# Token sums of a gated layer made in place, from the tile that the multiplication filled

## The chip, the cores and the metric

The kernel runs on one core of one Trainium2 chip. The metric is the time of one execution in microseconds (us); lower is better. Three runs of the kernel before gave 828.37, 828.44 and 830.95 us, median 828.44.

## The reference, cut to what matters

An attention over 32 memory slots for 4 batches of 576 tokens is followed by two feed-forward layers. All is float32.

```
x = attn_out as [2304 tokens, 512]
a = x @ w_a ; b = x @ w_b          # 512 -> 1536
x = (a * b) @ w_out                # 1536 -> 512   "the projection"
h = x @ w_in                       # 512 -> 2048
g = h * sigmoid(1.702 * h)
out = g @ w_out2                   # 2048 -> 512
```

The change is in what happens to `a * b` between its multiplication and the projection.

## The kernel before

**Engines and order.** TensorE (PE) does all products, each float32 operand split into a high and a low part and multiplied in three passes. ScalarE (ACT) and VectorE (DVE) empty the PSUM banks and decode weights (which come as raw 64-bit words); GpSimd (POOL) does elementwise sums beside DVE; SyncE (SP) issues nearly all DMAs. A planner (`Order`) runs while the program is built: it keeps a clock for each engine and for the DMA, starts from durations in `Lengths`, and writes each engine's instructions in the order in which its plan has them. Each engine, SP too, then works its list strictly in that order: an instruction that waits holds up all behind it.

**The gated layer** (`fold`, `gated`, `gated_out`). The 1536 columns are 6 groups `g` of 256, two blocks `j` of 128 each. For each group and batch, `fold` (L771) makes the effective weights; `gated` (L819) multiplies each half `u` (288 tokens) of the batch; ACT copies `a` from PSUM into a tile `gr` (L838), DVE multiplies `b` into it (L841), and SP stores the tile, 128 x 2 x 288, to a DRAM tensor `g1d` (L846). There are 24 pairs of group and batch and so 48 such stores. `gr` has four tiles of half a batch each.

**The token sums** (`sum_kept`, `sum_tokens`). The projection is one level of Strassen's scheme: 7 products in place of 8, over 2 x 2 blocks; one direction of the blocks is `j`, the other is a split of the tokens. The blocks of the token side are b11, b12, b21, b22; the products use b11, b21, b22 as they are, and four sums T1 to T4 of them. Before, the token split is between two stretches of 384 tokens within 768 (three such periods `p`). From the mark `close` on (the end of attention, near 142 us) `sum_kept` loads 2 x 768 tokens of a group from `g1d` into one of two tiles in `acc` (L924), POOL makes the four sums in place (L936), and SP stores them to `g1t` (L937). There are 18 such rounds. A load waits until its tile is free, that is until the store of the round two before it has landed.

**The projection** (`load_kept`, `split_kept`, `project`). For each period and product SP loads the block from `g1d` or `g1t` (L963), ACT and DVE or POOL split it into high and low parts, and PE multiplies (L1002). The weights for it come from `w_out`, of which 12 pieces are loaded into raw tiles (L360), decoded by ACT (L426) and DVE (L428, L430, L434), and combined (`combine_out`). Two raw tiles, `raw_74` and `raw_75` in the program, serve all weights after the end of attention.

**After it**: `w_in` (L1279), the gate, `w_out2` (L1480 and L1511).

Of the kernel before, what the change touches and what calls it, by code (L numbers as in the profile page):

```python
# [34 lines left out]
PS1 = 14.8  # L35
PT1 = 15
PB1 = 4
PI = 9
# [41 lines left out]
def pool(n):  # L80
    return 150 + 2.1 * n
# [18 lines left out]
class Order:  # L100
# [9 lines left out]
    def __init__(self):  # L110
        self.clock = {PE: 0.0, ACT: 0.0, DVE: 0.0, POOL: 0.0}
        self.dma, self.marks, self.streams, self.count = 2000.0, {}, [], 0

        self.handicap = {DVE: W0}

    def mark(self, t, *key):
        self.marks[key] = t

    def load(self, t, size, *key):

        self.dma = max(self.dma, t) + size / 385.0
        self.mark(self.dma + 2000.0, *key)

# [61 lines left out]
def tile_mem_attention_moe_moe2(  # L185
# [58 lines left out]

    g1d = dram.tile([F1, NT], F32, name="g1d")
    g1t = dram.tile([4 * F1 // 2, NT // 2], F32, name="g1t")
    g2d = dram.tile([F2, NT], F32, name="g2d")
# [5 lines left out]
    raw_s = slots(wp, 2, [P, 512, 2], "raw", U32)  # L253
    raw_t = list(raw_s.free)
    raw_x = slots(pa, 1, [P, 512, 2], "raw_x", U32)
# [7 lines left out]
    def y_of(p):  # L263
# [15 lines left out]
    ]  # L279
    gr_s = Slots([  # L280
        p2_m[:, o:o + G1 * U].rearrange("p (j t) -> p j t", j=G1)
        for o in range(B * HG * M, B * HG * M + 4 * G1 * U, G1 * U)
    ])
    rg_s, ring_s, sums_s, hc_s = Slots(), Slots(), Slots(), Slots()
    o1_s = {c: Slots() for c in range(F1 // P)}
# [59 lines left out]

    def raw_of(i):
        return raw_x if i == 2 * NHG - 1 else raw_s

# [358 lines left out]
    def close_attention():  # L707

        for n in range(NU):
            for e in range(2):  # L710
                yield "mark", "attn", n, e
        yield "mark", "raw_p"
        for i in range(4):
# [8 lines left out]
        four[0], four[1], four[2] = *views(spare, 4 * DM, 2), acc[:, 10 * DM:14 * DM]  # L722
        spare = views(spare, DM, NA * G1 + 2 * NHG)
        for c in range(NA * G1):
            give(o1_s[c], spare[c:c + 1])
        for r in range(2 * NHG):
            give(home[4, r], spare[NA * G1 + r:NA * G1 + r + 1])
        od.mark(now(), "close")

    py, pw, big = None, None, {}  # L730

    def room_late():

        for i in range(NA // 2):
            yield "mark", "w1", i
        yield "mark", "fold", 4, B - 1
        nonlocal pw
# [59 lines left out]
    def gated(g, b, u):  # L797
# [4 lines left out]
        e = eff_t[g, b][0]  # L802
        gr = yield "slot", gr_s
        left, pt, wide = [], [], have("close")
# [28 lines left out]
    def gated_out(g, b, u, j, pt, gr, left):  # L833
        (ta, pa_), (tb, pb) = pt
        n = j.stop - j.start
        xa, xb = (x[0][:, :, :U] if n > 1 else x[0][:, :U].rearrange("p (i t) -> p i t", i=1) for x in (pa_, pb))
        t, _ = yield ACT, max(ta, gr[1]), act(n * U, True)
        nc.scalar.activation(out=gr[0][:, j], in_=xa, func=AF.Copy)  # L838
        (pair_s if n > 1 else bank_m).release(pa_, t)
        t, _ = yield DVE, max(t, tb), dve(n * U)  # L840
        nc.vector.tensor_tensor(out=gr[0][:, j], in0=xb, in1=gr[0][:, j], op=ALU.mult)  # L841
# [68 lines left out]

    def kept(g, o, n):
        t = 0.0
        for i in range(o // U, (o + n - 1) // U + 1):
            t = max(t, (yield "mark", "g1", g, i // 2, i % 2))
        return t

    def sum_kept():

        yield "mark", "close"
        last = [(4, 0), (4, 1), (5, 0), (4, 2), (5, 1), (5, 2)]  # L920
        for g, p in [(g, p) for g in range(NG1 - 2) for p in range(NP)] + last:
                s = yield "slot", sums_s
                t = max(s[1], (yield from kept(g, 2 * p * N2, 2 * N2)))
# [4 lines left out]
                od.load(t, CW * 2 * N2 * 4, "kept", p, g)  # L928
                od.spawn(PT1 + 8 * p, sum_tokens(p, g, s))

    def sum_tokens(p, g, s):
        t = yield "mark", "kept", p, g
        b11, b12, b21, b22 = (s[0][:, i] for i in range(4))
        for dst, in0, in1 in ((b11, b12, b11), (b12, b22, b12), (b22, b22, b11), (b21, b21, b22)):
            t, _ = yield POOL, t, Lengths.pool * pool(N2)
            nc.gpsimd.tensor_tensor(out=dst, in0=in0, in1=in1, op=ALU.subtract)  # L936
        nc.sync.dma_start(  # L937
            out=g1t.rearrange("(x g p) t -> g p x t", g=NG1, p=P)[g][:, :, p * N2:(p + 1) * N2], in_=s[0]
        )
        sums_s.release(s, t + 2500.0)  # L940
        od.mark(t + 2500.0, "sums", p, g)

    def load_kept():

        for p in range(NP):
            for name in STEPS:
                b = PRODUCTS[name][1]
                for q in range(NG1 // 2):
                    s = yield "slot", rg_s
                    t = s[1]  # L950
                    for g in (2 * q, 2 * q + 1):
                        if b in PLAIN:
                            j, u = PLAIN[b]
                            o = (2 * p + u) * N2
                            t = max(t, (yield from kept(g, o, N2)))
                        else:
                            t = max(t, (yield "mark", "sums", p, g))
                    if b in PLAIN:
                        src = g1d.rearrange("(g j p) t -> j p g t", j=G1, p=P)[j]
                    else:  # L960
                        o = p * N2
                        src = g1t.rearrange("(x g p) t -> x p g t", g=NG1, p=P)[TSUM[b]]
                    nc.sync.dma_start(out=s[0], in_=src[:, 2 * q:2 * q + 2, o:o + N2])  # L963
                    od.load(t, CW * N2 * 4, "rg", p, name, q)
                    loaded["rg", p, name, q] = s
# [54 lines left out]
    def product_out(t, p, r, name, ps):  # L1020
# [13 lines left out]
        if p == 1:  # L1034
            for g in range(NG1):
                t = max(t, (yield "mark", "sums", NP - 1, g))
        mb = 2 * half + r
# [28 lines left out]
    WK, WB = NA * 2 * NB, 7 * (NG1 - NA) * 2 * NB + 128  # L1066
    PLAIN = {B11: (0, 0), B21: (1, 0), B22: (1, 1)}
    TSUM = {T1: 0, T3: 1, T4: 2, T2: 3}
    yc, win, wo2 = {}, {}, []
# [3 lines left out]
    def views(m, n, count, o=0):  # L1073
        return [m[:, o + i * n:o + (i + 1) * n] for i in range(count)]
# [18 lines left out]
    def room_weights():  # L1093

        yield "mark", "first"
        tiles = [x.rearrange("p (i t) -> p i t", i=4) for x in views(acc, 4 * N2, 2)]
        give(sums_s, tiles)
        yield "mark", "fold", 2, B - 1
# [20 lines left out]
    def room_buffers():  # L1119

        for b in range(B):
            for g in range(NG1):
                for u in range(2):
                    yield "mark", "g1", g, b, u
        give(hc_s, views(p2_m, N2, 7))
# [430 lines left out]
    def store(i, src, queues=(nc.sync,)):  # L1556

        for n, t in enumerate(range(i * P, (i + 1) * P, QP)):
            b, r = divmod(t, S)
            e, c = divmod(r // QP, QC // 2)  # L1560
# [17 lines left out]
    def main():  # L1578
# [4 lines left out]
        for p in range(NP):  # L1583
            yield from project(p)
        yield from quad(*order[0])
        room_projected()
        od.spawn(6, load_gated())
# [17 lines left out]
    with tc.manual_schedule():  # L1605
# [18 lines left out]
        od.spawn(9, room_weights())  # L1624
        od.spawn(3, sum_kept())
        od.spawn(3, load_kept())
# [39 lines left out]
```

## Time and profile before

| | |
|---|---|
| median of three runs | 828.44 us |
| the profiled execution | 830.54 us, of which the span of the profile is 828.7 us |
| PE busy | 763.5 us, 92% of the span |
| DVE, ACT, POOL busy | 609.5, 394.3, 378.5 us |
| moved by DMA | 171.23 MB, mean 207 GB/s |
| granted TensorE clock, mean | 0.965 |

Busy shares are averages over stages with different limits, so they say little alone. The stages are: attention with the first gated work (to 104 us), gated work with nothing in its way (104 to 142), gated work with the token sums and the weights of the projection (142 to 307), the start of the projection (307 to 344.4), and the rest.

### The profile page before, as it was taken

How to read it: one execution, taken by the hardware profiler on the slowest of the kernel's cores; microseconds unless marked ns; L12 is line 12 of the kernel's file. 1: busy time of each engine (PE TensorE's matmuls, PEld its weight loads, DVE VectorE, ACT ScalarE, POOL GpSimd, SP SyncE). 2: the span in 40 equal slices, each digit the busy share in tenths (PEclk: the TensorE clock that was granted, in tenths of full speed). 3: DMA queues.
4: the chain of work that ended last, by engine and by line, in shares of the span. 5: the costliest groups of instructions: out<-in, count | busy, mean ns of one | idle time of the engine just before them, and what ended most of it. 6: DMA issues, size and time to landing. Idle time of an engine off the chain costs nothing.

```text
span 828.7 us, 14577 instructions
## 1 busy us (share of the span) xinstructions
PE 763.5 (92%) x5360; PEld 701.3 (85%) x5360; DVE 609.5 (74%) x920; ACT 394.3 (48%) x781; POOL 378.5 (46%) x326
## 2 busy tenths in 40 slices
PE   8899999977876875799999999999999999999997
PEld 7667788766655775799999999999999888899997
DVE  4888987554765565359659897776778779999884
ACT  3565654322443242356466556555455446544441
POOL 0211100534656285539348977322214009887661
PEclk9999999988988987999999999999999999999999
DMA  8987735778766688975666255644457995754411
GB/s 255 314 273 237 247 122 162 257 260 264 261 207 207 205 311 273 319 245 167 199 187 185 62 172 207 195 166 161 155 194 263 298 316 186 231 168 131 130 33 40
DMA packets 115160, 171.23 MB, mean 207 GB/s; under 512 B 8592, under 2 KB 89232, under 8 KB 115088
## 3 DMA queue, kind: packets, MB, share of 16 engines
q1 hardware_dynamic: 109632, 160.89, 60.4%
q10 hardware_dynamic: 5456, 9.41, 3.3%
q8 instruction: 42, 0.69, 0.3%
q14 instruction: 30, 0.25, 0.1%
HBM read 114.16 MB, written 56.10 MB: 205 GB/s over the span
## 4 chain that ended last, share of the span: by engine, by line
PE 59%; DMA 16%; DVE 8%; POOL 8%; issue 4%; ACT 3%; SPq 2%; ACTq 0%; DVEq 0%; POOLq 0%
PE bank L1279 17%; PE bank L1511 12%; PE bank L1480 11%; PE bank L1002 10%; PE bank L819 5%; DMA g1t<-acc 4%; DMA raw<-in_moe_w_out_dram 4%; DMA raw<-in_moe_w_b_dram 3%; POOL acc L328 2%; POOL w L328 2%; DMA acc<-g1d 1%; POOL acc L936 1%; POOL w1b L328 1%; DMA phi<-in_phi_dram 1%; POOL attn L328 1%
## 5 line engine op out<-in xcount | busy, mean ns | idle before, releaser
L819 PEld LDWEIGHTS bank<-attn,eff 128*128 128x128 f32 x1152 | 166.2, 201 | 55.1 <-ACT gr L838 21.1
L819 PE MATMUL bank<-attn,eff 128*128 128x288 f32 x1152 | 179.3, 313 | 32.0 <-ACT gr L838 18.3
L936 POOL TENSOR_TENSOR acc<-acc 128x384 f32<-128x384 f32 x72 | 80.4, 1132 | 111.7 <-DMA acc<-g1d 109.8
L328 POOL TENSOR_TENSOR acc<-acc 128x512 f32<-128x512 f32 (+2 forms) x64 | 94.7, 1502 | 44.4 <-DVE w L328 25.6
L328 DVE TENSOR_TENSOR w<-acc,w 128x512 fp32r<-128x512 f32 (+2 forms) x101 | 103.8, 1055 | 11.1 <-ACT w L334 11.1
L1321 DVE TENSOR_TENSOR acc<-bank,acc 128x384 f32<-128x384 f32 x168 | 88.4, 550 | 31.6 <-PE bank L1279 19.8
L1002 PE MATMUL bank<-attn,w 128*128 128x384 f32 x504 | 97.1, 346 | 13.5 <-ACT attn L334 10.1
L1002 PEld LDWEIGHTS bank<-attn,w 128*128 128x128 f32 x504 | 90.8, 195 | 16.8 <-ACT attn L334 10.7
L334 ACT ACTIVATE w<-acc 128x512 fp32r<-128x512 f32 (+2 forms) x129 | 74.8, 590 | 56.1 <-PE bank L1511 37.1
L328 DVE TENSOR_TENSOR attn<-acc,attn 128x768 fp32r<-128x768 f32 (+3 forms) x59 | 72.8, 1248 | 35.1 <-ACT attn L334 34.6
L334 ACT ACTIVATE attn<-acc 128x768 fp32r<-128x768 f32 (+2 forms) x80 | 61.1, 768 | 54.9 <-PE bank L1002 27.0
L1331 ACT ACTIVATE acc<-acc 128x384 f32<-128x384 f32 x96 | 48.3, 521 | 47.6 <-DVE acc L1321 47.1
L328 POOL TENSOR_TENSOR attn<-acc,attn 128x768 fp32r<-128x768 f32 (+2 forms) x21 | 35.9, 1720 | 46.2 <-ACT attn L334 46.2
L1279 PE MATMUL bank<-attn,w 128*128 128x384 f32 x288 | 55.3, 334 | 0.7 <-POOL attn L328 0.7
L1279 PEld LDWEIGHTS bank<-attn,w 128*128 128x128 f32 x288 | 50.3, 188 | 1.1 <-POOL attn L328 1.1
L841 DVE TENSOR_TENSOR gr<-bank,gr 128x288 f32<-128x288 f32 (+1 forms) x64 | 38.4, 599 | 15.4 <-PE bank L819 12.8
L1002 PE MATMUL bank<-attn,w1b 128*128 128x384 f32 x252 | 47.9, 336 | 1.2 <-ACT attn L334 0.6
L426 ACT ACTIVATE acc<-raw 128x512 f32<-128x512 f32 x27 | 18.3, 678 | 61.3 <-DMA raw<-in_moe_w_b_dram 34.8
L838 ACT ACTIVATE gr<-bank 128x288 f32<-128x288 f32 (+1 forms) x64 | 33.6, 526 | 27.2 <-PE bank L819 26.8
L1279 PE MATMUL bank<-w1b,w 128*128 128x384 f32 x224 | 46.2, 334 | 0.0
L1002 PEld LDWEIGHTS bank<-attn,w1b 128*128 128x128 f32 x252 | 43.8, 188 | 2.3 <-DVE attn L328 1.4
L328 POOL TENSOR_TENSOR w<-acc,w 128x256 fp32r<-128x256 f32 (+2 forms) x26 | 28.4, 1102 | 36.0 <-ACT w L334 36.0
(177 smaller groups left out, 1456.5 us busy)
## 6 DMA issues: line engine op xcount, KB each, us to landing
g2d<-acc SPq DMA_DIRECT2D x96, 192.0 KB, 2.3
raw<-in_moe_w_out_dram SPq DMA_DIRECT2D x28, 512.0 KB, 5.3
g1d<-gr SPq DMA_DIRECT2D x48, 288.0 KB, 5.4
acc<-g1d SPq DMA_DIRECT2D x18, 768.0 KB, 4.8
g1t<-acc SPq DMA_DIRECT2D x18, 768.0 KB, 6.7
acc<-g1t SPq DMA_DIRECT2D x36, 384.0 KB, 3.7
acc<-g1d SPq DMA_DIRECT2D x27, 384.0 KB, 4.0
acc<-g2d SPq DMA_DIRECT2D x10, 1024.0 KB, 6.4
```

The lines of the kernel that those rows point to most:

```text
L328: (nc.gpsimd if e == POOL else nc.vector).tensor_tensor(out=dst, in0=in0, in1=in1, op=op)
L334: nc.scalar.activation(out=hi, in_=src, func=AF.Copy)
L819: nc.tensor.matmul(dst[:, :U], e[:, c, sw, i * CW + j * P:i * CW + (j + 1) * P], attn(b, mv, c, u * U, U), start=(n == 0), stop=(n == 3 * ...
L838: nc.scalar.activation(out=gr[0][:, j], in_=xa, func=AF.Copy)
L841: nc.vector.tensor_tensor(out=gr[0][:, j], in0=xb, in1=gr[0][:, j], op=ALU.mult)
L936: nc.gpsimd.tensor_tensor(out=dst, in0=in0, in1=in1, op=ALU.subtract)
L1002: nc.tensor.matmul(ps[0][:, :N2], w1_of(a, g, sw)[:, r * P:(r + 1) * P], b[0][:, mv, i], start=(first and q == n == 0), stop=(q == NG1 // ...
L1279: nc.tensor.matmul(ps[0][:, :N2], w[:, sw, r, :], y[mv][r], start=(n == 0), stop=(n == 5))
L1321: nc.vector.tensor_tensor(out=s[0], in0=ps[0][:, :N2], in1=x[0], op=ALU.add)
L1331: nc.scalar.activation(out=c[0], in_=c[0], func=AF.Gelu_apprx_sigmoid)
L1480: nc.tensor.matmul(ps[i, s][0], b[0][:, sw, c - o, :], wo2[c][:, mv], start=(c == n == 0), stop=(c == 4 * K4 - 1 and n == 2),)
L1511: nc.tensor.matmul(ps[name][0][:, :NB], x[0][:, sw, c, :], moving(b, h // 2 + c, mv), start=(h == c == n == 0), stop=(h > 0 and c == K4 - ...
```

## The change

The token blocks are now the two halves `u` of each batch: b11 and b12 are the two halves of block `j` = 0, b21 and b22 those of block `j` = 1. A tile `gr` holds both halves of a batch, 128 x 4 x 288, so that all four blocks of a group and batch stand side by side in it. After each half SP stores what the products use as it is: both blocks of the first half, and only b22 of the second (L869 of the changed kernel). Then POOL makes the four sums in that same tile (L884), and SP stores them (L885). `sum_kept` with its loads, and `g1t`, are gone; all seven blocks lie in `g1d`, 1152 tokens wide, and periods are stretches of 384 of those.

There are four tiles of a whole batch: two in the old place and two in the attention's pool, which are given up at its end (`gr_x`); two more come in `acc` when the first group is folded. Every third piece of `w_out` gets a third raw tile in `spare` (`raw_z`). The planner counts stores on its DMA clock too, and from `close` to the end of the projection it uses 330 bytes per ns and 3000 ns to landing (`RATE`) in place of 385 and 2000. The rows of the final stores follow the new token order.

```diff
+    gr_m = [p2_m[:, o:o + 4 * U] for o in range(B * HG * M, B * HG * M + 4 * G1 * U, 4 * U)]
+    gr_p = [pa.tile([P, 4 * U], F32, name=f"grp{i}") for i in range(2)]
+    gr_s = Slots([x.rearrange("p (i t) -> p i t", i=4) for x in gr_m + gr_p])
+    gr_x = list(gr_s.free[2:])
...
     def raw_of(i):
+        if pieces[i][0][0] == "o1" and i % 3 == 0:
+            return raw_z
...
-            o = b * S + u * U
+            lo, n = ((0, G1), (3, 1))[u]
             nc.sync.dma_start(
-                out=g1d[g * CW:(g + 1) * CW, o:o + U].rearrange("(j p) t -> p j t", p=P), in_=gr[0]
+                out=g1v[2 * u:2 * u + n, :, g, b * U:(b + 1) * U].rearrange("x p t -> p x t"),
+                in_=gr[0][:, lo:lo + n],
             )
-            gr_s.release(gr, t + 2500.0)
-            od.mark(t + 2500.0, "g1", g, b, u)
+            t = od.store(t, n * P * U * 4)
+            od.mark(t, "g1", g, b, u)
+            if u == 1:
+                od.spawn(PT1, sum_tokens(t, g, b, gr))
+
+    def sum_tokens(t, g, b, gr):
+        b11, b21, b12, b22 = (gr[0][:, i] for i in range(4))
+        for dst, in0, in1 in ((b11, b12, b11), (b12, b22, b12), (b22, b22, b11), (b21, b21, b22)):
+            t, _ = yield POOL, t, Lengths.pool * pool(U)
+            nc.gpsimd.tensor_tensor(out=dst, in0=in0, in1=in1, op=ALU.subtract)
+        nc.sync.dma_start(out=g1v[3:7, :, g, b * U:(b + 1) * U].rearrange("x p t -> p x t"), in_=gr[0])
+        t = od.store(t, 4 * P * U * 4)
...
+            gr_s.release(gr, t)
...
-    def sum_kept():
-        yield "mark", "close"
...
-                nc.sync.dma_start(
-                    out=s[0].rearrange("p (j u) t -> p j (u t)", j=G1),
-                    in_=g1d[g * CW:(g + 1) * CW, 2 * p * N2:2 * (p + 1) * N2].rearrange("(j p) t -> p j t", p=P),
-                )
...
-        give(sums_s, tiles)
+        give(gr_s, [x.rearrange("p (i t) -> p i t", i=4) for x in views(acc, 4 * U, 2)])
```

SP's list after the end of attention, before the change, where the first pieces of `w_out` are loaded (`g1d<-gr` stores a gated tile, `acc<-g1d` loads for a round of sums, `g1t<-acc` stores one):

```order
L846 DMA g1d<-gr 128x2x288 x2
L360 DMA raw_74<-in_moe_w_out_dram 128x1024
L937 DMA g1t<-acc 128x4x384
L924 DMA acc<-g1d 128x2x768
L846 DMA g1d<-gr 128x2x288
L937 DMA g1t<-acc 128x4x384
L924 DMA acc<-g1d 128x2x768
L360 DMA raw_75<-in_moe_w_out_dram 128x1024
L846 DMA g1d<-gr 128x2x288
L360 DMA raw_74<-in_moe_w_out_dram 128x1024
```

The same place of the changed kernel (L885 stores four sums, L869 plain blocks; `acc` is here a gated tile in `acc`, `spare` the third raw tile):

```order
L369 DMA raw_74<-in_moe_w_b_dram 128x512
L369 DMA spare<-in_moe_w_out_dram 128x1024
L885 DMA g1d<-acc 128x4x288
L869 DMA g1d<-gr 128x2x288
L369 DMA raw_73<-in_moe_w_out_dram 128x1024
L885 DMA g1d<-acc 128x4x288
L869 DMA g1d<-gr 128x288
L369 DMA raw_74<-in_moe_w_out_dram 128x1024
L869 DMA g1d<-gr 128x2x288
L369 DMA spare<-in_moe_w_out_dram 128x1024
```

The loads ahead of the sums are gone from between the raw loads; stores of sums remain between them.

POOL's list in the last third of attention, before (L328 on `sT` and `attn` is softmax work, L530 a copy that the transposes of the next heads need, L936 the sums):

```order
L328 TENSOR_TENSOR sT_108<-sT_108,sm_111 128x576
L530 COPY et_95<-phi_94 128x640
L328 TENSOR_TENSOR sT_109<-sT_109,sm_113 128x576 x2
L328 TENSOR_TENSOR sT_108<-sT_108,sm_112 128x576
L328 TENSOR_TENSOR attn_83<-aT_110,attn_83 128x576
L530 COPY et_95<-phi_93 128x640
L530 COPY et_95<-phi_94 128x640
L936 TENSOR_TENSOR acc<-acc 128x384 x32
```

And in the changed kernel (L335, L539 are the old L328, L530; L884 the sums):

```order
L335 TENSOR_TENSOR sT_109<-sT_109,sm_112 128x576
L539 COPY et_96<-phi_95 128x640
L335 TENSOR_TENSOR sT_110<-sT_110,sm_114 128x576
L884 TENSOR_TENSOR gr<-gr 128x288 x6
L335 TENSOR_TENSOR sT_109<-sT_109,sm_113 128x576
L884 TENSOR_TENSOR gr<-gr 128x288 x2
L884 TENSOR_TENSOR grp_88<-grp_88 128x288 x4
L884 TENSOR_TENSOR grp_89<-grp_89 128x288 x4
L539 COPY et_96<-phi_95 128x640
L335 TENSOR_TENSOR sT_110<-sT_110,sm_115 128x576
```

Sixteen sums, those of the first four tiles, now stand on POOL ahead of the last softmax work and of one copy for the transposes.

## Rows read from the trace of the kernel before

**Rows 1.** Busy time by stage: stretch, length, engines, granted clock, DMA share, GB/s.
```profile
core 0: us, PE busy (x) PEld busy (x) DVE busy (x) ACT busy (x) POOL busy (x), PEclk, DMA share, GB/s
62.00:104.00 42.00, 39.44 (x441) 32.61 (x426) 37.53 (x80) 25.17 (x61) 7.08 (x7) 1.00 0.75 243
104.00:142.00 38.00, 38.00 (x369) 32.42 (x367) 30.51 (x63) 20.10 (x45) 0.00 (x0) 1.00 0.38 131
142.00:307.00 165.00, 129.56 (x942) 109.71 (x941) 99.42 (x127) 54.20 (x96) 86.19 (x74) 0.88 0.75 247
307.00:344.40 37.40, 24.62 (x121) 22.61 (x120) 16.91 (x18) 11.51 (x18) 21.02 (x17) 0.86 0.82 280
344.40:828.70 484.30, 476.95 (x2868) 458.89 (x2868) 381.37 (x524) 251.89 (x484) 255.03 (x215) 1.00 0.57 181
```

**Rows 2.** Lines of PE, 142 to 345 us: count, busy us, mean ns, idle before.
```profile
L819 PE MATMUL bank<-attn,eff 128*128 128x288 f32 x717 | 114.2, 320 | 32.0 <-ACT gr L838 18.3 <-DVE eff L790 6.5 <-ACT eff L788 5.5
L1002 PE MATMUL bank<-attn,w 128*128 128x384 f32 x86 | 19.2, 379 | 11.9 <-ACT attn L334 10.1 <-DVE attn L328 1.8
L1002 PE MATMUL bank<-attn,w1b 128*128 128x384 f32 x36 | 7.1, 340 | 1.0 <-ACT attn L334 0.6 <-DVE attn L328 0.4
```

**Rows 3.** Timeline of PE at full clock, 122 to 131 us: start, us.
```profile
122.88 6.62 PE L819 MATMUL bank<-attn,eff 128*128 128x288 f32 x48
129.42 1.09 PE L771 MATMUL bank<-acc,gr 64*32 64x512 f32 x16
130.44 0.79 PE L819 MATMUL bank<-attn,eff 128*128 128x288 f32 x4
```

**Rows 4.** The same view, 350 to 358 us.
```profile
350.44 4.32 PE L1002 MATMUL bank<-attn,w 128*128 128x384 f32 x24
354.60 2.24 PE L1002 MATMUL bank<-attn,w1b 128*128 128x384 f32 x12
```

**Rows 5.** Waits of ACT, 140 to 345 us: total us, times, longest.
```profile
ACT spare L426 <- DMA raw<-in_moe_w_out_dram: 29.2, 8, 7.6
ACT acc L426 <- DMA raw<-in_moe_w_out_dram: 20.0, 4, 8.2
```

**Rows 6.** Waits of SP's list, 140 to 345 us.
```profile
SPq L924 <- DMA g1t<-acc: 88.7, 15, 8.9
SPq L846 <- DVE gr L841: 30.5, 9, 8.5
SPq L937 <- POOL acc L936: 18.4, 6, 3.9
```

**Rows 7.** The chain of waits, 176 to 200 us: start, us, what.
```profile
178.62 6.90 DMA g1t<-acc
...
185.54 0.36 SPq L924
...
185.99 5.81 DMA raw<-in_moe_w_out_dram
...
191.83 0.68 ACT spare L426
...
195.80 4.21 PE bank L819 x16
```

**Rows 8.** DMA issues of the whole run: count, KB each, median us to landing.
```profile
g1d<-gr SPq DMA_DIRECT2D x48, 288.0 KB, 5.4
...
acc<-g1d SPq DMA_DIRECT2D x18, 768.0 KB, 4.8
g1t<-acc SPq DMA_DIRECT2D x18, 768.0 KB, 6.7
```

**Rows 9.** Lines of POOL and DVE, 142 to 307 us.
```profile
L936 POOL TENSOR_TENSOR acc<-acc 128x384 f32<-128x384 f32 x57 | 62.4, 1111 | 104.6 <-DMA acc<-g1d 103.1
...
L430 DVE SCALAR_TENSOR_TENSOR acc<-raw,acc 128x512 uint32<-128x512 uint32 x8 | 8.5, 1062 | 0.2
```

**Rows 10.** The same DVE operation, 104 to 142 us.
```profile
L430 DVE SCALAR_TENSOR_TENSOR spare<-raw,spare 128x512 uint32<-128x512 uint32 x3 | 2.1, 686 | 0.0
```

**Rows 11.** Waits of POOL, 40 to 142 us.
```profile
POOL sT L328 <- DVE sm L654: 21.9, 3, 11.0
```

More of the change, by code (lines that the diff above doesn't have):

```diff
@@ L36 @@
 PT1 = 15
+RATE = 330.0, 3000.0
 PB1 = 4
@@ L114, in __init__ @@
         self.handicap = {DVE: W0}
+        self.rate, self.land = 385.0, 2000.0
     def mark(self, t, *key):
@@ L119, in load, with store @@
     def load(self, t, size, *key):
-        self.dma = max(self.dma, t) + size / 385.0
-        self.mark(self.dma + 2000.0, *key)
+        self.dma = max(self.dma, t) + size / self.rate
+        self.mark(self.dma + self.land, *key)
+    def store(self, t, size):
+        self.dma = max(self.dma, t) + size / self.rate
+        return self.dma + self.land
     def spawn(self, prio, stream):
@@ L243, in slots @@
         return Slots([pl.tile(shape, dt, name=f"{name}{i}") for i in range(n)])
-    g1d = dram.tile([F1, NT], F32, name="g1d")
-    g1t = dram.tile([4 * F1 // 2, NT // 2], F32, name="g1t")
+    g1d = dram.tile([7 * F1 // 2, NT // 2], F32, name="g1d")
+    g1v = g1d.rearrange("(x g p) t -> x p g t", g=NG1, p=P)
     g2d = dram.tile([F2, NT], F32, name="g2d")
@@ L253, in tile_mem_attention_moe_moe2 @@
     raw_s = slots(wp, 2, [P, 512, 2], "raw", U32)
-    raw_t = list(raw_s.free)
+    raw_t, raw_z = list(raw_s.free), Slots()
     raw_x = slots(pa, 1, [P, 512, 2], "raw_x", U32)
@@ L279, in tile_mem_attention_moe_moe2 @@
     ]
[L280 to L284, printed above, removed]
+    gr_m = [p2_m[:, o:o + 4 * U] for o in range(B * HG * M, B * HG * M + 4 * G1 * U, 4 * U)]
+    gr_p = [pa.tile([P, 4 * U], F32, name=f"grp{i}") for i in range(2)]
+    gr_s = Slots([x.rearrange("p (i t) -> p i t", i=4) for x in gr_m + gr_p])
+    gr_x = list(gr_s.free[2:])
+    rg_s, ring_s, hc_s = Slots(), Slots(), Slots()
     o1_s = {c: Slots() for c in range(F1 // P)}
@@ L712, in close_attention @@
         yield "mark", "raw_p"
+        od.mark(now(), "closing")
+        for i, x in enumerate(gr_x):
+            if any(x is y for y in gr_s.free):
+                gr_s.free.remove(x)
+                od.mark(x[1], "gr_x", i)
+        for i in range(2):
+            yield "mark", "gr_x", i
         for i in range(4):
@@ L722, in close_attention @@
         four[0], four[1], four[2] = *views(spare, 4 * DM, 2), acc[:, 10 * DM:14 * DM]
+        give(raw_z, [spare[:, 12 * DM:14 * DM].bitcast(U32).rearrange("p (f w) -> p f w", w=2)])
         spare = views(spare, DM, NA * G1 + 2 * NHG)
@@ L727, in close_attention @@
             give(home[4, r], spare[NA * G1 + r:NA * G1 + r + 1])
+        od.rate, od.land = RATE
         od.mark(now(), "close")
@@ L736, in room_late @@
         yield "mark", "fold", 4, B - 1
+        for c in range(F1 // P):
+            yield "mark", "decoded", ("o1", c), 0
         nonlocal pw
@@ L802, in gated @@
         e = eff_t[g, b][0]
-        gr = yield "slot", gr_s
+        if u == 0:
+            gr_t[g, b] = yield "slot", gr_s
+        gr = gr_t[g, b]
         left, pt, wide = [], [], have("close")
@@ L837, in gated_out @@
         t, _ = yield ACT, max(ta, gr[1]), act(n * U, True)
-        nc.scalar.activation(out=gr[0][:, j], in_=xa, func=AF.Copy)
+        dst = gr[0][:, u * G1 + j.start:u * G1 + j.stop]
+        nc.scalar.activation(out=dst, in_=xa, func=AF.Copy)
         (pair_s if n > 1 else bank_m).release(pa_, t)
         t, _ = yield DVE, max(t, tb), dve(n * U)
-        nc.vector.tensor_tensor(out=gr[0][:, j], in0=xb, in1=gr[0][:, j], op=ALU.mult)
+        nc.vector.tensor_tensor(out=dst, in0=xb, in1=dst, op=ALU.mult)
         (pair_s if n > 1 else bank_m).release(pb, t)
@@ L844, in gated_out @@
         if len(left) == G1 // n:
-            o = b * S + u * U
+            lo, n = ((0, G1), (3, 1))[u]
             nc.sync.dma_start(
-                out=g1d[g * CW:(g + 1) * CW, o:o + U].rearrange("(j p) t -> p j t", p=P), in_=gr[0]
-            )
-            gr_s.release(gr, t + 2500.0)
-            od.mark(t + 2500.0, "g1", g, b, u)
+                out=g1v[2 * u:2 * u + n, :, g, b * U:(b + 1) * U].rearrange("x p t -> p x t"),
+                in_=gr[0][:, lo:lo + n],
+            )
+            t = od.store(t, n * P * U * 4)
+            od.mark(t, "g1", g, b, u)
+            if u == 1:
+                od.spawn(PT1, sum_tokens(t, g, b, gr))
+    gr_t = {}
+    def sum_tokens(t, g, b, gr):
[5 more added lines that the diff above has]
+        t = od.store(t, 4 * P * U * 4)
+        if have("closing") and any(gr is x for x in gr_x):
+            od.mark(t, "gr_x", [gr is x for x in gr_x].index(True))
+        else:
+            gr_s.release(gr, t)
+        od.mark(t, "g1", g, b, 2)
     def have(*key):
@@ L909, in lend_ring @@
             give(ring_s, [x.rearrange("p (i j t) -> p i j t", i=2, j=G1) for x in big["ring"]])
[L911 to L915, printed above, removed]
-    def sum_kept():
-        yield "mark", "close"
[L920 to L923, printed above, removed]
-                nc.sync.dma_start(
-                    out=s[0].rearrange("p (j u) t -> p j (u t)", j=G1),
-                    in_=g1d[g * CW:(g + 1) * CW, 2 * p * N2:2 * (p + 1) * N2].rearrange("(j p) t -> p j t", p=P),
-                )
[L928 to L941, printed above, removed]
     def load_kept():
@@ L950, in load_kept @@
                     t = s[1]
[L951 to L963, printed above, removed]
+                    for i in range(p * N2 // U, ((p + 1) * N2 - 1) // U + 1):
+                        for g in (2 * q, 2 * q + 1):
+                            t = max(t, (yield "mark", "g1", g, i, (0, 0, 1, 2)[min(STORED[b], 3)]))
+                    nc.sync.dma_start(out=s[0], in_=g1v[STORED[b], :, 2 * q:2 * q + 2, p * N2:(p + 1) * N2])
                     od.load(t, CW * N2 * 4, "rg", p, name, q)
@@ L1035, in product_out @@
             for g in range(NG1):
-                t = max(t, (yield "mark", "sums", NP - 1, g))
+                t = max(t, (yield "mark", "g1", g, B - 1, 2))
         mb = 2 * half + r
@@ L1066, in tile_mem_attention_moe_moe2 @@
     WK, WB = NA * 2 * NB, 7 * (NG1 - NA) * 2 * NB + 128
-    PLAIN = {B11: (0, 0), B21: (1, 0), B22: (1, 1)}
-    TSUM = {T1: 0, T3: 1, T4: 2, T2: 3}
+    STORED = {B11: 0, B21: 1, B22: 2, T1: 3, T4: 4, T3: 5, T2: 6}
     yc, win, wo2 = {}, {}, []
@@ L1095, in room_weights @@
         yield "mark", "first"
-        tiles = [x.rearrange("p (i t) -> p i t", i=4) for x in views(acc, 4 * N2, 2)]
-        give(sums_s, tiles)
+        give(gr_s, [x.rearrange("p (i t) -> p i t", i=4) for x in views(acc, 4 * U, 2)])
         yield "mark", "fold", 2, B - 1
@@ L1122, in room_buffers @@
             for g in range(NG1):
-                for u in range(2):
+                for u in range(3):
                     yield "mark", "g1", g, b, u
@@ L1558, in store @@
         for n, t in enumerate(range(i * P, (i + 1) * P, QP)):
-            b, r = divmod(t, S)
+            p, x = divmod(t, 2 * N2)
+            u, x = divmod(x, N2)
+            b, r = divmod(p * N2 + x, U)
+            r += u * U
             e, c = divmod(r // QP, QC // 2)
@@ L1585, in main @@
         yield from quad(*order[0])
+        od.rate, od.land = 385.0, 2000.0
         room_projected()
```

1 line of the change is left out of this document (removed).

## The prediction

> **What bounds the kernel now.** I read the stages first, because 92% busy PE over the whole run hides where it is not busy. From 104 to 142 us PE is busy 38.0 of 38.0 us, and after 344.4 us 476.95 of 484.3; in both the granted clock is 1.00 [rows 1]. Between them, from 142 to 344.4 us, it is busy 129.56 + 24.62 = 154.2 of 202.4 us, at a granted clock of 0.88 and 0.86 [rows 1]. So PE is idle 48.2 us there, and part of its busy time runs at the lower of the clock's two levels (1.2 instead of 2.4 GHz), after gaps.
>
> What would the same work take without a gap? At full clock one group and batch, its 48 matmuls and a fold, goes from 122.88 to 130.44 us, 7.56 us [rows 3]. The stretch holds 717 such matmuls [rows 2], 14.94 groups: 112.9 us. The 86 + 36 = 122 projection matmuls [rows 2] take 4.16 us per 24 from start to start [rows 4]: 21.1 us. Together 134.0 us, so the stretch loses 202.4 - 134.0 = 68.4 us. That is the most that any change to its waits can give.
>
> Who holds PE up? Mostly ACT: it had not yet emptied a bank (L838, 18.3 us of PE's wait) or had not yet made effective weights (L788, 5.5, and through DVE 6.5) [rows 2]. ACT was late because it stood at a weight decode whose raw piece had not come: 29.2 + 20.0 us for `w_out` alone, up to 8.2 at a time [rows 5]. And the raw piece was late because SP had not issued its load: SP waits 88.7 us, 15 times, at L924 for a store of sums to land [rows 6]. One turn of this stands in the chain of waits [rows 7]: the store of sums issued at 178.62 takes 6.90 us; only then, at 185.54, goes the load that waits for its tile; the raw load behind it goes at 185.99 and takes 5.81; ACT decodes at 191.83, and PE goes on at 195.80. The raw load had to wait for nothing but its place in SP's list.
>
> **What the change removes.** All 18 loads at L924, 18 x 768 KB [rows 8], and a quarter of the 48 plain stores of 288 KB, since b12 is no longer stored: 13,824 + 3,456 KB = 17.7 MB of 171.23. POOL made 72 sums of 384 columns at 1.111 us [rows 9], 80 us; it makes 96 of 288, at three quarters of that 0.83 us, again 80 us (at an unchanged 1.11, the other bound, 107 us). Stores of sums are 24 of 576 KB for 18 of 768, the same bytes. So bytes and one wait go; work does not.
>
> The 88.7 us are 64% of what SP waits at the three rows (88.7 + 30.5 + 18.4 = 137.6 [rows 6]). The other two stay in another form: plain stores still wait for DVE, stores of sums for POOL. Nothing in the trace says how PE's loss divides over SP's waits. Bounds: none of the loss comes back (DMA loads arrive late for another reason), or all 68.4. I take the share of the waits: 0.64 x 68.4 = 44 us. Two edits help in the same direction and are not counted apart: the third raw tile, and a planner that places decodes later. What is late next is then the cycle of the raw tiles: two `w_b` pieces per 7.56 us of gated work, against a landing near 5.8 us [rows 7], the decode's 0.68 on ACT [rows 7] and three operations of up to 1.06 on DVE [rows 9], 9.7 us in all; a third tile relaxes this for `w_out` only.
>
> **What it adds.** First, a tile is held longer: from the first half's copy over its two halves (7.56), four sums (3.3 to 4.4) and a store's landing (6.7 [rows 8]), with some 2 us for ACT and DVE, 20 to 21 us. Four tiles last 4 x 7.56 = 30 us, so ACT should find a free one with 9 us to spare; price 0, and if POOL or SP runs 10 us late, what it is late beyond that.
>
> Second, sums move into attention, where POOL was nearly idle: 7.08 of 42 us and then 0 [rows 1]. Of the 96, 32 (eight tiles) stand on POOL ahead of the end of attention's work. That is 27 us (36 at the upper bound) of POOL beside a DVE that is busy 37.53 of 42 us [rows 1]. A DVE operation with two tensors in SBUF took 0.686 us while POOL was idle [rows 10] and 1.062 beside its sums [rows 9], 1.55 times as long. If a third of DVE's work in attention is of such kinds (my assumption; none and all of it would give 0 and 15), 27 us of company lengthen some 9 us of it by 5. I take 3, since DVE's slack before 104 us, 4.5 us [rows 1], hides a part. The Trainium skill's "GPSIMD Engine Reference", section "Specifications", says that GpSimd shares its SBUF interfaces with VectorE, with contention for DVE instructions of a two-port mode or with two SBUF inputs; it speaks against this change, and the two rows agree. By the rule the 3 us are due; by an earlier stage with idle POOL alone they would be 0.
>
> Third, a new wait: the third sum overwrites b22 and must wait until b22's store has read it. A plain store takes 5.4 us to land [rows 8]. Behind the four sums of the fourth tile stands, on POOL, a copy for the transposes of the next heads, which PE, by its order, reaches some 3 us after that tile's last matmul. DVE and ACT 1.5, store 5.4, two sums 1.7, copy 0.9 make 9.5: PE waits some 6 us, less what the store lands faster. Bounds 0 and 10; I take 5. The eight early stores of sums, 4.7 MB, fall partly between 104 and 142 us, where the DMA share is 0.38 [rows 1]; I count them at nothing for that reason. Without that cover they would be 4.7 MB at 243 GB/s [rows 1], 19 us of transfer, of which loads for attention would see a part.
>
> After 344.4 us nothing is added: PE has 7.35 us idle there in all [rows 1], and every engine starts from the projection's matmuls, so the stage moves forward whole.
>
> **Sum.** 44 - 3 - 5 = 36 us. The profiled execution took 830.5 us (span 828.7), so 794.5 in its terms; the median of the runs is 828.4, and I forecast 792.
>
> **Rivals.** *Nearly all comes back* (0.14): DMA is relieved so far that decodes never wait. For it: 10% fewer bytes, and all of the loss descends from late loads. Against it: two raw tiles, and plain stores that wait. 68.4 - 8 = 60 us: 768, and anything to 778.
>
> *A new wait takes its place* (0.17): stores of sums (L885) still stand between raw loads and wait for POOL, which waits for plain stores. In the stage there are 16, and if each holds SP for 3.1 us (18.4 / 6 [rows 6]), 49 us of SP's 88.7 come back; the net 39 of 137.6 give 0.28 x 68.4 = 19, less 8 early: 817, in the range 806 to 825. For it: 13,824 KB of stores stay [rows 8], at a landing that was already the longest. Against it: those stores wait for POOL, which in this stage had been idle over 100 us, waiting for loads that are gone [rows 9].
>
> *Slower* (0.07): the sums on POOL and their stores on SP lock attention. POOL waits up to 11.0 us for DVE before softmax work [rows 11]; a sum that waits there holds the store, the store holds SP, and SP the loads of keys and raw weights behind it. With four such stores among the loads of attention, at up to 11.0 + 4.4 us each, attention ends up to 60 us late. This decides if more than the 44 us are lost there; at 52 lost, 836. Against it: in that stretch POOL is free 35 of 42 us [rows 1].
>
> *No change* (0.02): raw loads arrive late by their own landing, and SP's place is not what counted: 828. That the change does not do what it says I exclude: the list of SP shows the loads gone.
>
> **How the numbers follow.** The forecast has 0.60, with its own range 780 to 806. The range 773 to 820 leaves out the better half of the second case (0.07), the upper end of the third (0.04), and the last two (0.09), 0.20 in all. Faster by over 0.3% (2.5 us, about what a measurement can tell here) are the first three, 0.91; slower 0.07; the same 0.02.
>
> **What would show it.** Right: no wait of SP for a store of sums to land; ACT's waits for `w_out` well under the 49 us; PE's idle time between 142 us and the steady part of the projection down from 48 to about 15 to 20, with a granted clock above 0.95; the steady part begins near 308 instead of 344. PE waits once for the transposes' copy near 95 us, and the stretch to 142 us grows by about 8. Wrong: SP waits as long at L885 for POOL; ACT waits at its gated copy for a tile; DVE or POOL sets PE's pace; or attention ends over 15 us late.

## The result and the profile after

Four runs of the changed kernel gave 762.59 to 768.24 us, median 765.9; four of the kernel before, median 829.06. The ratio is 0.9232, with a 95% interval of 0.9194 to 0.927: 63 us faster. The forecast was 792, 36 us faster, and its range ended at 773, so the direction was right and the gain 1.75 times what was forecast. The profiled execution took 765.62 us (span 763.8), 64.9 less than the one before in both terms.

Where did 64.9 us come from? The stages of the changed kernel (same columns as [rows 1]) are cut where the last gated matmul ends, 257.6 us, and where the 132nd matmul of the projection ends, 284.1:

```profile
core 0: us, PE busy (x) PEld busy (x) DVE busy (x) ACT busy (x) POOL busy (x), PEclk, DMA share, GB/s
62.00:104.00 42.00, 39.19 (x420) 33.30 (x421) 39.25 (x76) 24.45 (x60) 20.36 (x20) 1.00 0.78 249
104.00:142.00 38.00, 37.45 (x380) 31.64 (x371) 29.41 (x60) 18.16 (x43) 16.70 (x20) 1.00 0.51 174
142.00:257.60 115.60, 113.11 (x943) 98.14 (x942) 108.11 (x142) 61.22 (x106) 83.32 (x71) 1.00 0.70 226
257.60:284.10 26.50, 24.58 (x135) 22.66 (x134) 16.92 (x17) 10.21 (x14) 16.53 (x14) 1.00 0.94 315
284.10:763.80 479.70, 473.09 (x2857) 455.43 (x2856) 377.91 (x523) 251.11 (x481) 250.38 (x209) 1.00 0.56 176
```

The kernel before reaches the same matmul at 348.36 us (its gated work ended near 307):

```profile
307.00:348.36 41.36, 28.54 (x133) 26.04 (x133) 19.39 (x21) 13.57 (x20) 24.82 (x20) 0.83 0.85 288
348.36:828.70 480.34, 473.03 (x2857) 455.46 (x2856) 378.88 (x522) 249.83 (x481) 251.22 (x212) 1.00 0.57 179
```

The two kernels do the same 2857 matmuls behind that point, in 480.3 and 479.7 us. Ahead of it, 142 to the 132nd projection matmul took 206.4 us and now takes 142.1. So 64.3 of the 64.9 us are in the one stage that the prediction named. PE's busy time there fell too (129.56 us for 942 matmuls in [rows 1], now 113.11 for 943), because the granted clock is 1.00 where it was 0.88: with the gaps gone, PE no longer works a part of them at the lower of its two levels.

The waits of SP's list, 140 to 283 us, against [rows 6] (total us, times, longest):

```profile
SPq L869 <- DVE gr L864: 27.2, 14, 5.5
SPq L869 <- DVE acc L864: 23.1, 12, 4.7
SPq L963 <- DVE attn L335: 12.9, 9, 4.5
...
SPq L885 <- POOL acc L884: 5.0, 6, 1.3
SPq L885 <- POOL gr L884: 4.8, 5, 2.0
```

The 88.7 us of waits for stores of sums to land are gone; the one wait of SP for a store to land is now 1.2 us, at a load of the projection (L963). But SP waits *more* than before for DVE at the plain stores: 50.3 us for 30.5. ACT's waits for raw pieces of `w_out`, 49.2 us in [rows 5], and PE's longest wait in the stage:

```profile
ACT acc L435 <- DMA raw<-in_moe_w_b_dram: 2.9, 2, 2.0
ACT spare L435 <- DMA spare<-in_moe_w_out_dram: 1.7, 2, 1.4
...
ACT spare L435 <- DMA raw<-in_moe_w_out_dram: 1.2, 1, 1.2
```

```profile
PE bank L841 <- DVE acc L864: 1.7, 1, 1.7
```

ACT's `w_out` waits are 2.9 us in all and PE's idle time is 2.5 us in 115.6. DVE, busy 108.11 us of those, is now nearest behind PE.

How the raw loads moved is seen in a pair of rows. A raw tile is free when DVE has made the last decode operation on it (L434 before, L443 after); then SP may issue the next load into it. Before, DVE's timeline and SP's (start, us, what):

```profile
176.68 0.67 DVE L434 SCALAR_TENSOR_TENSOR acc<-raw,acc 128x512 uint32<-128x512 uint32 x1
```

```profile
185.99 0.42 SPq L360 DMA_DIRECT2D raw<-in_moe_w_out_dram  x1
```

After:

```profile
157.30 0.68 DVE L443 SCALAR_TENSOR_TENSOR spare<-raw,spare 128x512 uint32<-128x512 uint32 x1
```

```profile
158.04 0.33 SPq L369 DMA_DIRECT2D raw<-in_moe_w_a_dram  x1
```

Tile free at 177.35, load issued at 185.99: 8.6 us late. After: free at 157.98, issued at 158.04, 0.06 us. I call this the **lateness** of a load. I sum it over 16 raw loads that follow attention: the last two pairs of `w_a` and `w_b` pieces (a pair counts once), the twelve of `w_out` and the first two of `w_in`. The raw tiles are used in turn, so that with two tiles a load waits for the decode of the load two before it. The sum was 98.5 us before and is 1.6 us now (of 15 loads; nothing was in the third tile before its first).

### The profile page after: what moved, and what is told of

It is laid out like the page before. It is cut to its first block, busy times and chain, and to the rows that moved or that the text cites. A ratio compares the mean times of both kernels' runs of the same rounds, so it can differ in the third digit from the quotient of the medians.

```text
span 763.8 us, 14637 instructions
## 1 busy us (share of the span) xinstructions
PE 741.0 (97%) x5360; PEld 684.8 (90%) x5360; DVE 615.9 (81%) x926; ACT 396.9 (52%) x784; POOL 397.3 (52%) x347
## 2 busy tenths in 40 slices
DMA packets 110360, 153.54 MB, mean 201 GB/s; under 512 B 8400, under 2 KB 89040, under 8 KB 110288
## 4 chain that ended last, share of the span: by engine, by line
PE 70%; DVE 9%; DMA 7%; POOL 7%; issue 4%; ACT 2%; SPq 0%; ACTq 0%; DVEq 0%; POOLq 0%
PE bank L1277 23%; PE bank L1509 13%; PE bank L1478 11%; PE bank L1002 11%; PE bank L841 8%; POOL w L335 2%; DMA g1d<-grp 2%; PE bank L791 1%; DMA phi<-in_phi_dram 1%; DVE eff L810 1%; POOL acc L335 1%; DMA acc<-g1d 1%; POOL gr L884 1%; DVE attn L335 1%; DVE acc L439 1%
## 5 line engine op out<-in xcount | busy, mean ns | idle before, releaser
L841 PEld LDWEIGHTS bank<-attn,eff 128*128 128x128 f32 x1152 | 154.5, 188 | 21.2 <-issue 4.4
L841 PE MATMUL bank<-attn,eff 128*128 128x288 f32 x1152 | 165.3, 299 | 2.8 <-DVE acc L864 1.7
L335 POOL TENSOR_TENSOR acc<-acc 128x512 f32<-128x512 f32 (+2 forms) x65 | 95.7, 1494 | 45.0 <-DVE w L335 26.1
L335 DVE TENSOR_TENSOR w<-acc,w 128x512 fp32r<-128x512 f32 (+2 forms) x103 | 106.5, 1060 | 12.4 <-ACT w L341 12.4
L1002 PE MATMUL bank<-attn,w 128*128 128x384 f32 x504 | 93.3, 336 | 3.1 <-DVE attn L335 1.5
L335 DVE TENSOR_TENSOR attn<-acc,attn 128x768 fp32r<-128x768 f32 (+3 forms) x57 | 71.2, 1260 | 28.5 <-ACT attn L341 27.4
L1002 PEld LDWEIGHTS bank<-attn,w 128*128 128x128 f32 x504 | 87.3, 188 | 6.0 <-DVE attn L335 2.8
L884 POOL TENSOR_TENSOR gr<-gr 128x288 f32<-128x288 f32 x48 | 49.2, 1032 | 31.1 <-DMA g1d<-gr 20.1
L335 POOL TENSOR_TENSOR attn<-acc,attn 128x768 fp32r<-128x768 f32 (+2 forms) x23 | 39.0, 1702 | 47.0 <-ACT attn L341 46.9
L1277 PE MATMUL bank<-attn,w 128*128 128x384 f32 x288 | 55.1, 334 | 0.0
L1277 PEld LDWEIGHTS bank<-attn,w 128*128 128x128 f32 x288 | 50.4, 188 | 0.0
L335 POOL TENSOR_TENSOR w<-dm,w 128x256 fp32r<-128x256 f32 x31 | 26.9, 880 | 36.9 <-ACT w L341 36.9
L335 POOL TENSOR_TENSOR w<-acc,w 128x256 fp32r<-128x256 f32 (+2 forms) x24 | 27.4, 1154 | 34.1 <-ACT w L341 34.1
L1277 PE MATMUL bank<-w 128*128 128x384 f32 x224 | 43.8, 334 | 0.0
L1277 PEld LDWEIGHTS bank<-w1b,w 128*128 128x128 f32 x224 | 39.5, 188 | 0.0
```

What stands on the lines that cost most here:

```text
L335: (nc.gpsimd if e == POOL else nc.vector).tensor_tensor(out=dst, in0=in0, in1=in1, op=op)
L841: nc.tensor.matmul(dst[:, :U], e[:, c, sw, i * CW + j * P:i * CW + (j + 1) * P], attn(b, mv, c, u * U, U), start=(n == 0), stop=(n == 3 * ...
L1002: nc.tensor.matmul(ps[0][:, :N2], w1_of(a, g, sw)[:, r * P:(r + 1) * P], b[0][:, mv, i], start=(first and q == n == 0), stop=(q == NG1 // ...
L1277: nc.tensor.matmul(ps[0][:, :N2], w[:, sw, r, :], y[mv][r], start=(n == 0), stop=(n == 5))
```

## The experiments

After the result two theories stood for the size of the gain. **A**: what held PE up was SP, standing in its strict list until a store of sums had landed, with raw loads behind it that were free to go. **B**: the 17.7 MB less (153.54 for 171.23 MB) make transfers land sooner. The other parts of the change (third raw tile, `RATE`, sums in place) might each have a share; the expectations call the first two of these **C**.

**Putting SP's wait back into the changed kernel.** Behind each store of sums SP issues a load of 64 bytes per partition from what was just stored, so that it stands until the store has landed.

```diff
         nc.sync.dma_start(out=g1v[3:7, ...], in_=gr[0])
+        nc.sync.dma_start(out=mark_, in_=g1v[3, :, g, b * U:b * U + 16])
```

> The changed kernel, and behind each store of four sums SP issues a tiny load (64 bytes per partition) of what was just stored, so that SP must stand until that store has landed, as it did before the change; no other work is added and the planned order is the same. Theory A (what counted was SP's place: it stood for stores of sums to land while raw weight loads queued behind it): some 16 stores between 142 us and the projection, 5 to 6 us each, are 80 to 95 us of SP's waits again, ACT waits for raw pieces again, and the time goes back to 805 to 830. Theory B (bytes: 17.7 MB fewer made every transfer earlier): no bytes come back, so 764 to 770. Theory C (the third raw tile and the planner's later decodes did it): 764 to 772.

Measured: 802.68 us, ratio 0.967 (0.962 to 0.9721); 37 us of the 63 are lost with hardly a byte added. SP's waits, 140 to 345 us:

```profile
SPq L887 <- DMA g1d<-acc: 38.3, 8, 6.9
SPq L887 <- DMA g1d<-gr: 33.7, 8, 6.7
```

It fell a little short of what A expected. With the load only after the end of attention (`if have("close")` ahead of it):

> As the first experiment, but SP stands for the store of sums only from the end of attention on, where the kernel before had its sums. Theory A (SP's place in the stage after attention): nearly all of the 37 us of the first experiment stay, since its gated work was 3 us late at 138 us and 23 us late at its end: 793 to 804. Rival (SP standing within attention did it): 768 to 780.

790.44 us, 0.9505 (0.9464 to 0.9546), with 79.2 us of such waits: between the two expectations, nearer to A. So 12 of the 37 us come from standing in attention, and 79 us of standing behind it cost 24.5 us here. The total of a wait says little about its price.

**Putting bytes back.** Each store of sums is issued a second time, into a DRAM tensor that nobody reads: 14.2 MB.

```diff
+        nc.sync.dma_start(out=g1w[0:4, :, g, b * U:(b + 1) * U].rearrange("x p t -> p x t"), in_=gr[0])
```

> The changed kernel, and each store of four sums is issued twice, the second time to a DRAM tensor that nobody reads: 24 x 576 KB, 14.2 of the 17.7 MB that the change saved, come back, as writes in place of reads, with no wait of SP for a landing. Theory A: SP is not held, so 766 to 775. Theory B: the DMA is as loaded as before and most of the gain goes, 810 to 825. Theory C: 766 to 772.

780.62 us, 0.9417 (0.9375 to 0.9459). Neither theory's number: 15 us, much less than B wanted, and more than A. Loads of `w_out` from 142 to 300 us (count, KB each, median us to landing), first in the changed kernel and then here:

```profile
raw<-in_moe_w_out_dram SPq DMA_DIRECT2D x8, 512.0 KB, 4.8
```

```profile
raw<-in_moe_w_out_dram SPq DMA_DIRECT2D x8, 512.0 KB, 6.8
```

They go out as promptly as in the changed kernel (late by 4.7 us in all), but land 2.0 us later. Yet little of the time is lost where they land. The same 48 matmuls beside attention that the changed kernel starts at 123.21 us start here at 131.37, and three groups later it is 159.66 for 146.77:

```profile
131.37 6.62 PE L843 MATMUL bank<-attn,eff 128*128 128x288 f32 x48
...
155.06 3.11 PE L843 MATMUL bank<-attn,eff 128*128 128x288 f32 x12 [3.39 <-ACT gr L863]
158.10 1.63 PE L793 MATMUL bank<-acc,gr 64*32 64x512 f32 x16
159.66 6.62 PE L843 MATMUL bank<-attn,eff 128*128 128x288 f32 x48
```

```profile
ACT spare L437 <- DMA g1d<-gr: 3.8, 1, 3.8
```

8.2 us were lost in attention and 4.7 more near 155 us, where ACT waited 3.8 us for a store to land, ahead of a decode, and PE for ACT. From there to the group that starts at 237.20 (223.66 in the changed kernel), the time in which `w_out` is loaded, it is 0.6 us; the rest, some 6 us up to the 132nd projection matmul, comes behind it. This execution took 785.15 us, the slowest of four, and 8 us in attention were once lost without any added bytes (below). So the 15 us are measured, but their way is not shown, and it is not mainly the later landing of `w_out`.

**The third raw tile and the rates.** Both undone in the changed kernel; the tile alone; the rates alone (5 rounds):

```diff
-RATE = 330.0, 3000.0
+RATE = 385.0, 2000.0
...
-        if pieces[i][0][0] == "o1" and i % 3 == 0:
-            return raw_z
```

> The changed kernel without its third raw tile and with the planner's old rates (385 bytes per ns, 2000 ns to landing): only the sums in place remain. Theory A: 766 to 776, since raw loads still go out in time. Theory B: 766 to 776. Theory C: the decodes are paced by two tiles and planned too early again, 790 to 815.

> The changed kernel without its third raw tile, with the planner's new rates. Together with old rates it cost 5.4 us. If the tile is what that was: 770 to 773. If the rates were: 764 to 767.

> The changed kernel with its third raw tile and the planner's old rates. Without the tile it was 769.3, without tile and new rates 771.3. If tile and rates are worth 3 and 2 us on their own: 767 to 769. If the tile only pays with the new rates: 770 to 773.

Both: 771.31 us, 0.9303 (0.9266 to 0.9339), as A and B expected and not C. Without the third tile: 769.28, 0.9252 (0.9223 to 0.9282). With the old rates: 774.24, 0.9328 (0.9293 to 0.9363). These two lie outside the ranges expected, the first by 1 us below that of the tile, the second by 1 us above. The tile is worth some 3 us, both together some 5. That the tile with old rates comes out no better than neither is not settled: in its profiled run (779.75 us, the slowest of six) the timeline of PE shows the gated work beside attention 8 us later than in the changed kernel, though its list of instructions up to there is the same:

```profile
131.17 6.66 PE L841 MATMUL bank<-attn,eff 128*128 128x288 f32 x48
```

The changed kernel starts these 48 matmuls at 123.21 us. That is before the edit can act, so it varies between executions, and the 3 us of the rates stay open.

**Moving the wait in the kernel before.** If SP's place in the list is what counts, the wait should be harmless on another engine. Only the loads at L924 moved to POOL's list; then those and the stores at L937:

```diff
-                nc.sync.dma_start(
+                nc.gpsimd.dma_start(
```

> The kernel before the change, with one edit: the 18 loads for the sums are issued by POOL, whose sums need them anyway, and not by SP. Bytes, rounds, tiles, raw tiles and the planner's rates are those of before. POOL now stands for the store of sums to land. Theory A: SP is free, raw loads go out in time, and 30 to 60 us come back: 770 to 800. Theory B: 825 to 832. Theory C: 825 to 832.

848.64 us, 1.0228 (1.0193 to 1.0262): slower, the expectation missed.

> The kernel before the change, with loads and stores of the token sums both issued by POOL: SP has nothing to do with the sums any more, and bytes, rounds, tiles and rates are those of before. Theory A: raw loads go out as soon as their tile is free, and the gated work ends at 255 to 275 us instead of 307; but POOL's rounds still take some 8.7 us each, as when only the loads were there, so sums end near 300 and the projection waits for them: 785 to 815 in all. Theory B (bytes): gated work ends near 300, time 820 to 832.

858.47 us, 1.0332 (1.03 to 1.0365): missed again. The waits of POOL and SP with the loads moved, and of POOL with both moved:

```profile
POOL acc L924 <- DMA g1t<-acc: 50.8, 10, 7.4
```

```profile
SPq L937 <- POOL acc L936: 90.0, 13, 11.2
```

```profile
POOL acc L924 <- DMA g1t<-acc: 67.2, 13, 8.3
```

The wait only moved. POOL stood for the stores instead of making sums; in the first kernel the sums came late, SP waited 90.0 us for them at L937, and its 16 raw loads were late by 90.9 us. In the second SP is free, and the 16 raw loads are late by 1.3 us in all, as A says; but POOL's list also holds parts of the projection's weights (L328), for which ACT waits up to 38.1 us at a time, and PE pays there. ACT's wait, and PE's timeline near 242 us:

```profile
ACT w L334 <- POOL spare L328: 42.0, 4, 38.1
```

```profile
242.42 9.17 PE L819 MATMUL bank<-attn,eff 128*128 128x288 f32 x48 [35.70 <-DVE eff L790]
```

PE stood 35.7 us at one place. These two can't tell A from B. They agree with the view that the price of a wait is what stands behind it, on whichever list.

**Changing only the order in the kernel before.** The wait stays on SP and no byte is saved, but the planner may place the next round's load only 2 us after its slot is free in the plan, so it stands later in SP's list, behind raw loads:

```diff
                 s = yield "slot", sums_s
+                yield "when", lambda: now() >= s[1] + 2000.0 or None
```

> The kernel before the change with one edit: the load of a round of sums takes its place in SP's list only 2 us of plan after its tile's planned release, so that SP stands less for the store to land. Bytes, tiles, rounds and rates as before; rounds move later, five fewer are loaded before the projection's first operand. Theory A: lateness of the raw loads well under 98 us, gated work ends before 290 instead of 307; the projection may wait longer for sums, so 795 to 825 in all. Rival (bytes, or the round's own length): gated work ends at 300 or later, 826 to 840.

807.58 us, 0.9722 (0.9682 to 0.9761): 23 us from a line that changes only the order. SP's waits, 140 to 345 us:

```profile
SPq L846 <- DVE gr L841: 46.4, 22, 6.6
SPq L938 <- POOL acc L937: 33.7, 10, 7.1
...
SPq L925 <- DMA g1t<-acc: 9.2, 6, 3.4
```

9.2 us for stores of sums in place of 88.7, and the 16 raw loads are late by 3.9 us in all. The gated work ends at 277.4 us instead of near 307, a gain of 30. Then the sums, made later, are late for the projection: ACT waits 30.0 us for them, up to 19.3 at a time, which gives a part back.

```profile
ACT attn L334 <- DMA acc<-g1t: 30.0, 6, 19.3
```

But prompt raw loads are not all of it. The changed kernel with two tiles and the old rates has them too (2.2 us in all), and ends its gated work at 259.4 us, 18 us before this one. This kernel has the bytes of before: its twelve `w_out` loads land in 6.0 us (median) where they take 4.0 there. No run here isolates what these 18 us are.

**All parts back but the sums in place.** The changed kernel with SP standing and the sums stored twice (both from `close` on), two raw tiles and the old rates:

> The changed kernel with all that came back singly put back together after the end of attention: SP stands for each store of sums, each store of sums is issued twice (about 16 x 576 KB), no third raw tile, old planner rates. What stays of the change is that sums start in attention and that the load for them (a wait of POOL) is gone. If the parts add up (34 for standing, 10 for two thirds of the bytes, 5 for raw tile and rates): 812 to 820. If they feed each other, as one queue's lateness does: 820 to 832. If they share one cause, 800 to 810.

801.86 us, 0.9641 (0.9604 to 0.9678), some 10 below the range for parts that add up. But that range took standing at 34 us; with the 24.5 that it cost after attention, 10 for the bytes and 5 for tile and rates, the parts add up to some 805. SP stood for stores of sums for 65.0 us, not 88.7, and the lateness was 34.1 us, a third of what it had been before. So one more kernel, in which SP also waits for the tiny load itself, by storing it:

```diff
+            nc.sync.dma_start(out=g1m, in_=mark_)
```

> The sixth experiment (SP stands for each store of sums after attention, bytes twice, two raw tiles, old rates; 802 us), and SP also stores the tiny tile that it loaded, so that it stands for the tiny load's landing too, some 2 us more at each of 16 places. In the kernel before a raw load stood, with its tile free, 98 us in all (16 loads after the end of attention), in the sixth experiment 51, in the eighth about 3; the times are 829, 802 and 769, 0.6 us of time per us of that lateness. Theory A, now with that number: the lateness grows by 25 to 50 us and the time with it to 815 to 832. Rival (the last 27 us belong to the load for the sums and its wait on POOL, not to SP): 800 to 810.

831.57 us, ratio 1.0013 (0.9985 to 1.004): the time of the kernel before, with sums in place and their loads gone.

```profile
SPq L891 <- DMA g1d<-gr: 32.0, 8, 5.5
SPq L891 <- DMA g1d<-acc: 31.6, 8, 5.6
SPq L892 <- DMA mark<-g1d: 26.1, 16, 3.3
```

89.7 us of standing for 88.7, lateness 69.3 for 98.5, the gated work ends at 302.4, and ACT waits again:

```profile
ACT spare L437 <- DMA raw<-in_moe_w_out_dram: 39.7, 7, 10.8
```

Against the kernel above it differs by one store of 8 KB per round, and by 30 us. That the time is that of the kernel before is in part chance: it reaches the 132nd projection matmul at 339.4 us, 9 earlier, and takes 488.0 us from there, 8 more. None of these kernels beats the changed one.

The kernels with two raw tiles, by lateness of the 16 raw loads (issue less the end of the tile's last decode operation, both from the timelines):

| kernel | lateness, us | time, us |
|---|---|---|
| before, load later in the list | 3.9 | 807.6 |
| changed, two tiles | 5.1 | 769.3 |
| all back but the sums | 34.1 | 801.9 |
| the same, standing longer | 69.3 | 831.6 |
| before | 98.5 | 829.1 |

(The expectation of the last experiment has 51 for the third row. Two loads in a row can stand in one line of the timeline, as x2; counted singly they give 34.1.) Lateness does not price the loss by itself. Between the third and the fourth row, which differ by the standing alone, 35.2 us of it go with 29.7 us of time. Between the last and the first, which differ by the order alone, 94.6 us go and only 23 us of time with them. The first two rows are equally prompt and 38 us apart: the first moves more bytes and waits for its sums.

## Why the prediction was right and wrong

**The stage and its loss: right.** It put the loss at 68.4 us between 142 and 344.4 us. 64.3 came back. By the same counting (134.0 us, and 2.1 for the 12 matmuls up to 348.36) 142.1 us now lose 6.

**The mechanism: right, and shown for a part of the gain.** SP at L924, the raw load behind it, ACT, PE, as in [rows 7]. Order alone, in the kernel before, gave 23 us; standing alone, put back after attention in the changed kernel, took 24.5 away. All of the gain went only with standing, bytes, two tiles and old rates together.

**The size: wrong, at one step.** "I take the share of the waits: 0.64 x 68.4 = 44 us." It takes the wait of a list to be a budget of which each row costs its part. The runs show that it isn't. The other rows did not keep their 24 of the 68.4 us: the one for plain stores grew (L869, 50.3 us where 30.5 were), and PE is idle for 2.5 us in the 115.6 of the gated stretch, so they cost next to nothing. There SP follows DVE, which follows PE, and no raw load whose tile is free stands behind: the raw loads are late by 1.6 us in all. The wait at L924 followed a transfer, with ready loads behind it. Nor was that row worth its 44 us by itself: its order alone gave 23 (30 by the end of the gated work). The rest came with what else the change removed, and no run divides it. So "nearly all comes back", 768 us, was the case, for which I gave two raw tiles and plain stores that wait as the arguments against.

**Bytes: left out as such.** The 17.7 MB were counted as removed and priced at nothing. 14.2 MB put back by themselves cost 15 us, by a way that is not shown. After attention, standing (24.5), bytes (some 10) and tile and rates (5) add up to 40 us, and together they took 36. The 30 us more of the last kernel came with 25 us more of standing. How the 63 us of the change itself divide between standing, bytes and sums that come in time stays open.

**Costs of the early sums: 8 forecast, none seen.** The gated work beside attention starts its 48 matmuls at 123.21 us for 122.88 in [rows 3]; this compares two executions, and such a start can be 8 us later in another (131.17 above):

```profile
123.21 6.62 PE L841 MATMUL bank<-attn,eff 128*128 128x288 f32 x48
```

The first part of it, 3 us for POOL beside DVE, had the right cause. The operation of 675 ns before (62 to 104 us) did grow; lines of DVE, before and then after:

```profile
L434 DVE SCALAR_TENSOR_TENSOR acc<-raw,acc 128x512 uint32<-128x512 uint32 x7 | 4.7, 675 | 0.0
```

```profile
L443 DVE SCALAR_TENSOR_TENSOR acc<-raw,acc 128x512 uint32<-128x512 uint32 x7 | 7.1, 1013 | 0.1
```

1.5 times as long. DVE's busy time grew by only 1.7 us, from 37.53 [rows 1] to 39.25 of 42, and its slack hid that. The Trainium skill's "GPSIMD Engine Reference", section "Specifications", names contention for DVE instructions with two SBUF inputs; these rows agree with it. The second part, 5 us for b22's store ahead of the transposes' copy, had a wait that came and did not count. POOL's timeline:

```profile
90.67 4.20 POOL L884 TENSOR_TENSOR grp<-grp 128x288 f32<-128x288 f32 x4 [4.00 <-DMA g1d<-grp]
95.24 2.52 POOL L884 TENSOR_TENSOR grp<-grp 128x288 f32<-128x288 f32 x2 [0.38 <-DMA g1d<-grp]
102.39 0.72 POOL L539 COPY et<-phi 128x640 f32<-128x640 f32 x1 [4.63 <-DMA phi<-in_phi_dram]
```

POOL waited 4.00 us for a plain store; yet the copy started at 102.39, 4.6 us after the sums, because it waited for its own load (issued at 95.66 us).

**The tile held longer, at nothing: right.** Neither PE nor ACT has a wait of note for a free tile. **The downstream stage moves forward whole: right**, to 0.6 us (480.3 and 479.7). **A new wait at L885 takes its place: wrong**, 9.8 us instead of the 49 of that rival. **Slower: wrong**; the stores of sums did not lock attention.

## What to carry to other kernels

The waits of an in-order list are not shares of a loss. For each, ask what stands behind it that could go already: list when the buffer of the next transfer came free and when the transfer was issued, and sum that lateness. It shows whether the list holds transfers up, not what that costs: here 94.6 us less of it gave 23 us. A wait with nothing ready behind it cost next to nothing (50.3 us of them), and one that follows a transfer's landing should come after all issues that are ready; moving it to another engine's list made this kernel slower twice, because that list held needed work.

## What the runs showed of the hardware

A load of 512 KB landed in 4.8 us (median) where the DMA share was 0.70 (142 to 257.6 us of the changed kernel), and in 6.8 us with 14.2 MB more stored over the run.

An issue of a 768 KB load by POOL is an instruction on POOL, 0.72 us each (142 to 300 us, with only the loads moved):

```profile
L924 POOL DMA_DIRECT2D acc<-g1d x12 | 8.7, 723 | 58.3 <-DMA g1t<-acc 34.0 <-issue 19.1 <-DMA g1d<-gr 5.2
```

Two kernels with one list of instructions up to that point reached the same matmul beside attention 8 us apart (123.21 and 131.17).
